# The two float16 parts of the attention maxima: converted from SBUF and turned by VectorE's 32x32 transposition, in place of a TensorE product into a score bank

## The chip, the cores and the metric

The kernel runs on one core of a Trainium2 chip. Such a core has five engines that run side by side, each with its own queue of instructions, and they wait for each other through semaphores: TensorE (PE, matrix products; its weight loads are listed as PEld), VectorE (DVE), ScalarE (ACT), GpSimd (POOL) and SyncE (SP), which here issues all DMAs. SBUF is the on-chip memory of 128 partitions. PSUM holds TensorE's results in eight banks of 128 partitions by 512 float32. The metric is the device time of one launch in microseconds (us), the median of several runs; less is better.

## The reference

One transformer block in its parallel form, for a sequence of 2048 rows of width 512, with 32 heads of 16 dimensions and a hidden width of 1792:

```python
xn = _layernorm(x, axis=-1)
# attention
qkv = (xn @ wqkv)                       # split into q, k, v of 32 heads of 16
scores = einsum("bhqd,bhkd->bhqk", q, k) * (16 ** -0.5)
p = softmax(scores, axis=-1)
attn = einsum("bhqk,bhkd->bhqd", p, v)  # heads side by side again, then @ wo
# dense part
h = gelu(xn @ w1 + b1)
mlp = h @ w2 + b2
return x + attn_out + mlp
```

The softmax needs, for each query and head, the maximum of its 2048 scores before the exponentials can be taken. It is that maximum which the change concerns.

## The kernel before

Products in float32 accuracy are made of float16 parts: a value is split into a high part and the rest, and three products (high x high, high x rest, rest x high) are added up. For attention, `kst` and `qst` hold, for each head, a stack of 64 rows: 48 rows of such parts (16 dimensions, three each), and at the end rows 62 and 63. In `kst` these two rows hold the constant 1024 (`MROW`). In `qst` they hold, for each query, the high and the low float16 part of -maximum / 1024. So a product over all 64 rows is the score less the maximum of its query, and a product over the first 62 rows is the score alone.

The work of attention is cut into 32 tiles t: a group g of 4 heads (`NG` = 8) by a block qb of 512 queries (`NQB` = 4). A tile is worked in 16 units, and a unit is the step of the outer loop (`unit`). In each unit the kernel works at three places at once:

- `s_half` (L169 by way of `tiled`, and L257), four times a unit, for unit u: 128 queries by 512 keys of one head. The 62-row product goes into one of three score banks (tag S, name `pS`), and VectorE takes its maximum over the keys into a column of `mt`. These banks are used in turn. A fourth block waits until the reduction of the first has ended.
- `e_half` (L169, L302), four times a unit, for unit u - 19 (`LEAD`): 128 keys by 512 queries of one head, the 64-row product into a bank of tag T (name `pT`), and ScalarE takes its exponential into `pe`.
- `v_half` (L169) for a unit a little further back: the product of the exponentials with v, into `pV`. Beside it, `dense` runs some products of the projections or of the dense part, into `pD`. Both use one half of TensorE's rows each.

When the last of the 16 units of a tile is done, `s_end` reduces `mt` (64 values a query partition) to `mneg`, 16 columns (4 heads by 4 blocks of 128 queries): the negative maxima, with the queries on the partitions (L268). They are needed with the queries along the free dimension, in rows 62 and 63 of `qst`, three units later, when `e_half` comes to this tile. The way there is `store`, which runs in the middle of the next unit, after its first two score blocks and first `v_half`: TensorE multiplies `mneg` with a unit matrix (L275), which turns it, into a score bank taken with `banks("S")`; VectorE makes the high part and the rest from PSUM (`mhl`, L278 and L279); two DMAs write them to `m_d` in DRAM (L282) and four DMAs read them into the rows of `qst`, one for each head (L287). `mneg` has 32 columns for this product, of which 16 are cleared once at the start by GpSimd.

From the second tile on, all queues keep the order in which the code writes the instructions (`manual_schedule`). Ahead of it, for the layer norm, the first projections and the score blocks of the first tile, a scheduler orders them. Work that should come some units later is put into `queue` by `later`, and `tick` runs it at a unit's end. GpSimd's work goes through `pooled` and a budget of time for each unit: among it the normalisation of a finished tile (L358 to L360) and the pieces of the GELU (L1019 to L1027), which read and write SBUF. SyncE's queue, too, is in order: a DMA whose source isn't ready holds all that come behind it.

Of the kernel before, what the change touches and what calls it, by code (L numbers as in the profile page):

```python
# [8 lines left out]
F32 = mybir.dt.float32  # L9
F16 = mybir.dt.float16  # L10
I32 = mybir.dt.int32
AF = mybir.ActivationFunctionType
ALU = mybir.AluOpType
AX = mybir.AxisListType
# [3 lines left out]
P = 128  # L18
S = 2048
# [8 lines left out]
NQB = S // QB  # L28
NG = H // 4
# [13 lines left out]
MROW = 1024.0  # L43
# [4 lines left out]
def layer_kernel(ctx: ExitStack, tc: tile.TileContext, x, wqkv, wo, w1, b1, w2, b2, out):  # L48
    nc = tc.nc
    x = x.flatten_outer_dims()  # L50
    out = out.flatten_outer_dims()

    def pool(stack, name, bufs=1, space=None, side=None):
        kw = {k: v for k, v in (("space", space), ("side", side)) if v is not None}
        return stack.enter_context(tc.tile_pool(name=name, bufs=bufs, **kw))

    const = pool(ctx, "const")
    work = pool(ctx, "work")
    ps = pool(ctx, "ps", space=PSUM)
    dram = pool(ctx, "dram", space=DRAM)  # L60
# [4 lines left out]
    w1_d = dram.tile([NF // 2, P, 2, 2, NC, P], F16, name="w1_d")  # L65
    w2_d = dram.tile([P, 2, NF, D], F16, name="w2_d")
    acc_d = dram.tile([S, D], F32, name="acc_d")
    m_d = dram.tile([NG * NQB, 16, 2, P], F16, name="m_d")
    ot_d = dram.tile([D, 2, S], F16, name="ot_d")
    den_d = dram.tile([NG * NQB, 2, 4, QB], F32, name="den_d")  # L70

# [1 line left out]
    ident = const.tile([P, P], F32, name="ident")  # L73
# [19 lines left out]
    nc.gpsimd.memset(vv[:, :, H * VW:], 0.0)  # L93
    wo_s = const.tile([P, 2, NC, D], F16, name="wo_s")
    sexp = const.tile([P, 4], F32, name="sexp")

    mnegs = [const.tile([P, 32], F32, name=f"mneg{i}") for i in range(2)]
    for m in mnegs:
        nc.gpsimd.memset(m, 0.0)


    free_banks = {"S": [0, 1, 2], "T": [3, 4, 5], "D": [6], "V": [7]}
# [1 line left out]
    def bank_tile(k, tag):  # L104
        return ps.tile([P, QB], F32, tag=f"B{k}", bufs=1, name="p" + tag)

    def banks(tag):
        k = free_banks[tag].pop(0)
        free_banks[tag].append(k)
        return bank_tile(k, tag)  # L110
# [48 lines left out]
    def given(engine, ns):  # L159
        backlog[engine] += ns  # L160
# [17 lines left out]
    def leave(user, goes_on):  # L178

        p = newest.pop(user, None)  # L180
        if p is not None and goes_on:
            p.then_inc(turns, 1)
            tc.no_tile_sem_insts.add(p.ins.name)
            counted[0] += 1
            left.append(p)

    def enter():

        if left:
            goal[0] = f"turn{counted[0]}"  # L190
            for p in left:
                tc.add_to_no_dep_group(goal[0], p.ins)
            left.clear()
# [9 lines left out]
    def fetch_scale(m):  # L203

        scale_of[m] = nc.scalar.alloc_register(f"sexp{m}")
        nc.scalar.reg_load(scale_of[m], sexp[0:1, m:m + 1].bitcast(I32))

    mt_of, ptiles, pv_of, stores = {}, {}, {}, {}
    queue, slot = [], [0]

    def later(n, fn, local=False):
# [21 lines left out]
    def tick():  # L233
        run_due()
        run_steps()
        slot[0] += 1
# [8 lines left out]
    def s_half(u, n):  # L245

        t, i = divmod(u, 16)
        g, qb = divmod(t, NQB)
        qt, kb = divmod(i, 4) if t else (i % 4, i // 4)
        if t not in mt_of:  # L250
            mt_of[t] = work.tile([P, 4, 4, 4], F32, name="mt", bufs=2)
        ks, qs = kst[g % 2], qst[g % 2]
        p, a = divmod(n, 2)
        r = slice(64 * a, 64 * a + 62)
        s = banks("S")
        tiled(None, s, qs[p][qb][r, qt * P:(qt + 1) * P], ks[p][kb][r, :], True, True)
        nc.vector.reduce_max(mt_of[t][:, n, qt, kb:kb + 1], s, axis=AX.X)  # L257
        given("dve", 600)

    def s_end(u):  # L260

        t, i = divmod(u, 16)
        if i < 15:
            return
        g, qb = divmod(t, NQB)
        qs = qst[g % 2]
        mneg = mnegs[t % 2]
        nc.vector.tensor_reduce(mneg[:, :16], mt_of[t].rearrange("p h t k -> p (h t) k"), axis=AX.X, op=ALU.max, negate=True)  # L268
        given("dve", 220)

        def store():

            pt = banks("S")
            for a in range(2):
                nc.tensor.matmul(pt[32 * a:32 * a + 32, :64], mneg[64 * a:64 * a + 64, :],  # L275
                                 ident[64 * a:64 * a + 64, 64 * a:64 * a + 64], start=True, stop=True)
            mhl = work.tile([64, 2, 64], F16, name="mhl", bufs=2)
            nc.vector.tensor_scalar_mul(mhl[:, 0], pt[:64, :64], 1.0 / MROW)  # L278
            nc.vector.scalar_tensor_tensor(mhl[:, 1], pt[:64, :64], 1.0 / MROW, mhl[:, 0], op0=ALU.mult, op1=ALU.subtract)  # L279
            given("dve", 300)  # L280
            for a in range(2):
                nc.sync.dma_start(m_d[t, :, :, 64 * a:64 * a + 64], mhl[32 * a:32 * a + 16])  # L282
            for p in range(2):
                for a in range(2):
                    h = 2 * p + a
                    dst = qs[p][qb][64 * a + 62:64 * a + 64, :].rearrange("r (t q) -> r t q", q=P)
                    nc.sync.dma_start(dst, m_d[t, 4 * h:4 * h + 4].rearrange("t r q -> r t q"))  # L287

        stores[t] = store

    def e_half(u, n):

        p, a = divmod(n, 2)
        t, kt = divmod(u, 16)
        g, qb = divmod(t, NQB)
        st = banks("T")
        r = slice(64 * a, 64 * a + 64)
        k0 = (kt % 4) * P
        tiled(None, st, kst[g % 2][p][kt // 4][r, k0:k0 + P], qst[g % 2][p][qb][r, :], True, True)
        pe = work.tile([P, QB], F32, name="pe", bufs=12)  # L300
        ptiles[u, n] = pe
        nc.scalar.activation(pe, st, AF.Exp, scale=scale_of[g // 2])  # L302
        given("act", 520)

    def v_half(u, a):

        t, kt = divmod(u, 16)
        g, qb = divmod(t, NQB)
        if kt == 0 and a == 0:
            pv_of[t] = hold("V", "S")  # L310
        pv = pv_of[t][0]
        r = slice(64 * a, 64 * a + 64)
        for h in (2, 3, 0, 1):
            c = (4 * g + h) * VW
            product("V", pv[32 * h:32 * h + 32, :], vv[r, kt, c:c + 32], ptiles[u, h][r],
                    start=(kt == 0 and a == 0), stop=(kt == 15 and a == 1))
# [249 lines left out]
    def burst(gen, n):  # L566

        while n > 0 and (f := group(gen)) is not None:
            if not f.usable():
                break  # L570
            f.product(2)
            n -= 1
            ended()

    def dense(gen, side):

        f = group(gen)
        for _ in range(0 if f is None else f.pace[pos[0] % 2]):
            if not f.usable(side):
                return  # L580
            f.product(side)
# [25 lines left out]
    def spare(gen, side):  # L607

        if extra[0] is None and not spent[0]:
            f = next(gen, 0)  # L610
            spent[0] = f == 0
            extra[0] = Halves(f) if f else None
        if extra[0] is not None:
            extra[0].product(side)
            if extra[0].at == extra[0].n:
                extra[0] = None
# [16 lines left out]
    def unit(gen):  # L633


        u = pos[0]
        e = u - LEAD
        if e >= 0 and e % (2 * NQB * 16) == 0 and e < NU:
            fetch_scale(e // (2 * NQB * 16))
        if u == LEAD and cur[0] is not None:  # L640
            burst(gen, cur[0].left())
        pos[0] += 1
        for a in range(2):
            for b in range(2 * a, 2 * a + 2):
                if u < NU:
                    s_half(u, b)
                elif u > NU:
                    spare(gen, b % 2)
                if 0 <= e < NU:
                    e_half(e, b ^ 1)  # L650
            if u < LEAD:
                burst(gen, LFILL[u - 16] // 2)
            if e >= 0:
                enter()

                w, r = (e - 2, 1) if a == 0 else (e - 1, 0)
                live = 0 <= w < NU
                new = r == 0 and w % 16 == 0
                if live and not new:
                    v_half(w, r)  # L660
                dense(gen, 1 - r)
                if live and new:
                    v_half(w, r)

                for user, goes_on in (("V", live and not (r == 1 and w % 16 == 15)),
                                      ("D", cur[0] is not None and not cur[0].over())):
                    leave(user, goes_on)
                for k in backlog:
                    backlog[k] = max(0, backlog[k] - HALF)
                if live and r == 1:  # L670
                    v_end(w)
                ended()

            if a == 0 and u % 16 == 0 and u // 16 - 1 in stores:
                stores.pop(u // 16 - 1)()
        if u < NU:
            s_end(u)
        tick()
# [549 lines left out]
```

## Time and profile before

| | |
|---|---|
| median of 3 runs | 1525.09 us (1520.38 to 1526.5) |
| the profiled execution, its own time | 1520.55 us |
| span of its profile | 1518.8 us |
| busy: TensorE, VectorE, ScalarE, GpSimd | 1489.5, 1402.2, 1245.6, 664.5 us |
| mean granted TensorE clock | 0.996 of full speed |
| L257, the reductions of score blocks | 2048 of 684 ns |
| L268, L278, L279 on VectorE, 32 each | 219, 209, 217 ns |
| L275 on TensorE, 128 instructions | 216 ns |
| DMA: share of 16 engines' span | 25.4% |

A row of the groups names the line of the code, the engine, the operation, what is written from what, the shape and the count; then the busy time in us and the mean of one in ns; then the engine's idle time just before, with what ended it. Busy times overlap: the next instruction of an engine may start before the last one is recorded as ended, so that the sum of the durations is more than the busy time. A row of the timeline gives the start and the length in us, and in square brackets the idle time ahead of it and what ended it. "x2" says that neighbouring instructions of one kind are merged into one row.

### The profile page before, as it was taken

Reading aid. Unit: us, or ns where it says so; the run is one execution under the profiler, and the core shown is the slowest. Engines: PE = TensorE matmul, PEld = TensorE weight load, DVE = VectorE, ACT = ScalarE, POOL = GpSimd, SP = SyncE. Lnnn points to the kernel's source line nnn. Section 1 sums busy time; section 2 is a strip of 40 time slices with the busy share of each in tenths; the row PEclk is TensorE's granted clock in tenths of the full one; section 3 lists DMA queues with packets and bytes.
Section 4 is the critical chain, followed back from the end, with each engine's and each line's share of the span. In section 5 each row is a group of like instructions: output and inputs, shape, how many; then the busy total and the mean of one; then the engine's idle time right before and its main releaser. Section 6 shows DMA issues by size and latency. Waiting matters only on the chain.

```text
span 1518.8 us, 86848 instructions
## 1 busy us (share of the span) xinstructions
PE 1489.5 (98%) x39407; PEld 815.9 (54%) x39407; DVE 1402.2 (92%) x2367; ACT 1245.6 (82%) x2318; POOL 664.5 (44%) x686
## 2 busy tenths in 40 slices
PE   8999999999999999999999999999999999999998
PEld 3434555555555555555555555555555555555553
DVE  7899989999999999999999999999999999999933
ACT  5327778899988888898888898988888898888884
POOL 4113597547771112777411167751116775211110
PEclk9999999999999999999999999999999999999998
DMA  6454567542122201121011211122101201121422
GB/s 208 127 155 158 166 219 211 180 126 77 58 69 66 61 26 42 36 84 50 23 49 41 66 42 40 36 78 63 34 25 56 77 27 29 50 60 50 136 65 95
DMA packets 113674, 123.76 MB, mean 81 GB/s; under 512 B 24988, under 2 KB 85276, under 8 KB 113304
## 3 DMA queue, kind: packets, MB, share of 16 engines
q1 hardware_dynamic: 113304, 118.21, 25.4%
q8 instruction: 308, 5.05, 1.4%
q14 instruction: 62, 0.51, 0.1%
HBM read 80.61 MB, written 37.34 MB: 78 GB/s over the span
## 4 chain that ended last, share of the span: by engine, by line
PE 79%; DVE 16%; issue 2%; ACT 2%; DMA 1%; POOL 0%; SPq 0%; POOLq 0%
PE pV L169 23%; PE pD L169 19%; PE pT L169 17%; PE pS L169 16%; DVE mt L257 13%; PE pT L435 1%; PE pD L435 1%; DVE amx L709 1%; ACT pe L302 1%; ACT t L1014 1%; PE pT L528 1%; PE pV L528 0%; DMA m_d<-mhl 0%; DMA xs<-in_A_x_dram 0%; DMA wch<-in_B_w_dram 0%
## 5 line engine op out<-in xcount | busy, mean ns | idle before, releaser
L257 DVE TENSOR_REDUCE mt<-pS 128x1 f32<-128x512 f32 x2048 | 1304.5, 684 | 52.5 <-PE pS L169 34.8
L302 ACT ACTIVATE pe<-pT 128x512 f32<-128x512 f32 x2048 | 1100.8, 599 | 162.9 <-PE pS L169 78.6
L169 PE MATMUL pV<-pe,vv 64*32 64x512 f32 x8192 | 1076.3, 595 | 0.1
L169 PE MATMUL pT<-qst,kst 64*32 64x512 f16 x8192 | 718.3, 378 | 8.8 <-ACT pe L302 7.9
L169 PE MATMUL pS<-kst,qst 62*32 62x512 f16 x8192 | 624.3, 378 | 5.2 <-DVE mt L257 3.6
L169 PEld LDWEIGHTS <-kst 64*32 64x32 f16 x8192 | 285.7, 91 | 203.9 <-issue 103.6
L169 PEld LDWEIGHTS <-qst 62*32 62x32 f16 x8192 | 273.3, 92 | 206.3 <-issue 58.2
L169 PE MATMUL pD<-w_s,g 64*32 64x512 f16 x5376 | 364.6, 376 | 0.0
L169 PE MATMUL pD<-xb,wc 64*32 64x512 f16 x5376 | 360.9, 377 | 0.0
L169 PEld LDWEIGHTS pV<-pe,vv 64*32 64x32 f32 x8192 | 181.0, 105 | 88.3 <-PE pV L169 4.3
L1070 POOL TENSOR_TENSOR xa<-xa,yt 128x512 f32<-128x512 f32 x16 | 20.5, 1282 | 319.0 <-ACT yt L1068 319.0
L169 PEld LDWEIGHTS <-wc 64*32 64x32 f16 x5376 | 116.9, 91 | 41.6
L169 PEld LDWEIGHTS <-g 64*32 64x32 f16 x5376 | 112.2, 91 | 45.3
L169 PE MATMUL pD<-xt,wqk_h 64*32 64x512 f16 x2016 | 134.7, 377 | 1.7 <-issue 1.5
L1025 POOL TENSOR_TENSOR t<-hh 128x512 f32<-128x512 f32 x56 | 58.3, 1041 | 132.7 <-ACT hh L1045 121.8
L358 POOL TENSOR_TENSOR osb<-osb,rb 128x512 f32<-128x512 f32 x31 | 39.9, 1287 | 135.1 <-DMA rb<-den_d 76.0
L1027 POOL TENSOR_TENSOR t<-t,hh 128x512 f32<-128x512 f32 x56 | 71.9, 1284 | 4.7
L1020 POOL TENSOR_TENSOR t<-t,hh 128x512 f32<-128x512 f32 x56 | 71.8, 1281 | 4.7
L1022 POOL TENSOR_TENSOR g<-t,g 128x512 f16<-128x512 f32 x56 | 65.2, 1165 | 4.7
L169 PEld LDWEIGHTS <-wqk_h 64*32 64x32 f16 x2016 | 47.5, 92 | 23.4 <-issue 6.2
L169 PE MATMUL pD<-wo_s,oc 64*32 64x512 f16 x828 | 54.5, 378 | 0.0
L1045 ACT ACTIVATE hh<-pD,b_s,fac 128x512 f32<-128x512 f32 x56 | 43.6, 779 | 9.4 <-PE pT L169 3.3
(141 smaller groups left out, 862.4 us busy)
## 6 DMA issues: line engine op xcount, KB each, us to landing
wch<-in_B_w_dram SPq DMA_DIRECT2D x28, 512.0 KB
wc<-w_d SPq DMA_DIRECT2D x56, 256.0 KB
qk_d<-stg SPq DMA_DIRECT2D x32, 256.0 KB
rb<-den_d SPq DMA_DIRECT2D x124, 64.0 KB
w_d<-wsp SPq DMA_DIRECT2D x28, 256.0 KB
kst<-qk_d SPq DMA_DIRECT2D x128, 48.0 KB
qst<-qk_d SPq DMA_DIRECT2D x128, 48.0 KB
xs<-in_A_x_dram SPq DMA_DIRECT2D x16, 256.0 KB
```

The costliest lines, as they stand in the source:

```text
L169: p = nc.tensor.matmul(*args, **kw)
L257: nc.vector.reduce_max(mt_of[t][:, n, qt, kb:kb + 1], s, axis=AX.X)
L302: nc.scalar.activation(pe, st, AF.Exp, scale=scale_of[g // 2])
L358: pooled((1280, lambda: nc.gpsimd.tensor_tensor(osb, osb, rb, op=ALU.mult)), (620, lambda: nc.gpsimd.tensor_scalar(ot[:, 0], osb, 1.0, 0.0 ...
L435: nc.tensor.matmul(self.bank, lhs, rhs, start=start, stop=self.last and self.over())
L528: nc.tensor.matmul(pj, xt[:, i, c, t * P:(t + 1) * P], wh[j][:, c, :], start=(n == 0), stop=(n == 11))
L1020: (1280, lambda: nc.gpsimd.tensor_tensor(t1, t1, hh, op=ALU.mult)),
L1022: (1160, lambda: nc.gpsimd.tensor_tensor(g[:, 1, f, :], t1, g[:, 0, f, :], op=ALU.subtract)),
L1025: pooled((1040, lambda: nc.gpsimd.tensor_tensor(t1, hh, hh, op=ALU.mult)), (620, lambda: nc.gpsimd.tensor_scalar(t1, t1, 1.0, 1.0 / GELU_A ...
L1027: (1280, lambda: nc.gpsimd.tensor_tensor(t1, t1, hh, op=ALU.mult)),
L1045: nc.scalar.activation(hh, hp, AF.Identity, scale=scale, bias=bias)
L1070: add = lambda: nc.gpsimd.tensor_tensor(xa, xa, yt, op=ALU.add)
```

## The change

`mneg` has 16 columns only and comes from the working pool, in two buffers. Directly behind the reduction L268, in `s_end`, VectorE makes the two float16 parts from `mneg` in SBUF: the high part into columns 0 to 15 of `mh`, the rest into columns 16 to 31. Then VectorE transposes `mh` in blocks of 32 by 32, so that each block of 32 partitions (32 queries) of `mc` holds 32 rows (2 parts by 16 columns) by 32 queries. Four DMAs, one for each such block, write them to `m_d`, whose layout is now part, column, query; and four DMAs read them into `qst`, each now two rows of 512 in one piece. The DMAs are put on SyncE's queue at the same place, ahead of what `tick` issues at that unit's end. The product with the unit matrix, its score bank, the function `store` and its call in the middle of the next unit go, and so do GpSimd's two clearings.

```diff
--- before.py
+++ after.py
@@ -65,7 +65,7 @@
     w1_d = dram.tile([NF // 2, P, 2, 2, NC, P], F16, name="w1_d")
     w2_d = dram.tile([P, 2, NF, D], F16, name="w2_d")
     acc_d = dram.tile([S, D], F32, name="acc_d")
-    m_d = dram.tile([NG * NQB, 16, 2, P], F16, name="m_d")
+    m_d = dram.tile([NG * NQB, 2, 16, P], F16, name="m_d")
     ot_d = dram.tile([D, 2, S], F16, name="ot_d")
     den_d = dram.tile([NG * NQB, 2, 4, QB], F32, name="den_d")
 
@@ -93,10 +93,6 @@
     nc.gpsimd.memset(vv[:, :, H * VW:], 0.0)
     wo_s = const.tile([P, 2, NC, D], F16, name="wo_s")
     sexp = const.tile([P, 4], F32, name="sexp")
-
-    mnegs = [const.tile([P, 32], F32, name=f"mneg{i}") for i in range(2)]
-    for m in mnegs:
-        nc.gpsimd.memset(m, 0.0)
 
 
     free_banks = {"S": [0, 1, 2], "T": [3, 4, 5], "D": [6], "V": [7]}
@@ -205,7 +201,7 @@
         scale_of[m] = nc.scalar.alloc_register(f"sexp{m}")
         nc.scalar.reg_load(scale_of[m], sexp[0:1, m:m + 1].bitcast(I32))
 
-    mt_of, ptiles, pv_of, stores = {}, {}, {}, {}
+    mt_of, ptiles, pv_of = {}, {}, {}
     queue, slot = [], [0]
 
     def later(n, fn, local=False):
@@ -264,29 +260,22 @@
             return
         g, qb = divmod(t, NQB)
         qs = qst[g % 2]
-        mneg = mnegs[t % 2]
-        nc.vector.tensor_reduce(mneg[:, :16], mt_of[t].rearrange("p h t k -> p (h t) k"), axis=AX.X, op=ALU.max, negate=True)
+        mneg = work.tile([P, 16], F32, name="mneg", bufs=2)
+        nc.vector.tensor_reduce(mneg, mt_of[t].rearrange("p h t k -> p (h t) k"), axis=AX.X, op=ALU.max, negate=True)
         given("dve", 220)
 
-        def store():
-
-            pt = banks("S")
+        mh, mc = (work.tile([P, 32], F16, name=x, bufs=2) for x in ("mh", "mc"))
+        nc.vector.tensor_scalar_mul(mh[:, :16], mneg, 1.0 / MROW)
+        nc.vector.scalar_tensor_tensor(mh[:, 16:], mneg, 1.0 / MROW, mh[:, :16], op0=ALU.mult, op1=ALU.subtract)
+        nc.vector.transpose(mc, mh)
+        rows = m_d[t].rearrange("j c q -> (j c) q")
+        for b in range(4):
+            nc.sync.dma_start(rows[:, 32 * b:32 * b + 32], mc[32 * b:32 * b + 32])
+        for p in range(2):
             for a in range(2):
-                nc.tensor.matmul(pt[32 * a:32 * a + 32, :64], mneg[64 * a:64 * a + 64, :],
-                                 ident[64 * a:64 * a + 64, 64 * a:64 * a + 64], start=True, stop=True)
-            mhl = work.tile([64, 2, 64], F16, name="mhl", bufs=2)
-            nc.vector.tensor_scalar_mul(mhl[:, 0], pt[:64, :64], 1.0 / MROW)
-            nc.vector.scalar_tensor_tensor(mhl[:, 1], pt[:64, :64], 1.0 / MROW, mhl[:, 0], op0=ALU.mult, op1=ALU.subtract)
-            given("dve", 300)
-            for a in range(2):
-                nc.sync.dma_start(m_d[t, :, :, 64 * a:64 * a + 64], mhl[32 * a:32 * a + 16])
-            for p in range(2):
-                for a in range(2):
-                    h = 2 * p + a
-                    dst = qs[p][qb][64 * a + 62:64 * a + 64, :].rearrange("r (t q) -> r t q", q=P)
-                    nc.sync.dma_start(dst, m_d[t, 4 * h:4 * h + 4].rearrange("t r q -> r t q"))
-
-        stores[t] = store
+                h = 2 * p + a
+                nc.sync.dma_start(qs[p][qb][64 * a + 62:64 * a + 64, :],
+                                  m_d[t, :, 4 * h:4 * h + 4].rearrange("j t q -> j (t q)"))
 
     def e_half(u, n):
 
@@ -671,8 +660,6 @@
                     v_end(w)
                 ended()
 
-            if a == 0 and u % 16 == 0 and u // 16 - 1 in stores:
-                stores.pop(u // 16 - 1)()
         if u < NU:
             s_end(u)
         tick()
```

## The prediction

> **What bounds the kernel now.** I read the page's head first, then its chain of waits and the costliest groups.
>
> ```profile
> span 1518.8 us, 86848 instructions
> PE 1489.5 (98%) x39407; PEld 815.9 (54%) x39407; DVE 1402.2 (92%) x2367; ACT 1245.6 (82%) x2318; POOL 664.5 (44%) x686
> PE 79%; DVE 16%; issue 2%; ACT 2%; DMA 1%; POOL 0%; SPq 0%; POOLq 0%
> L257 DVE TENSOR_REDUCE mt<-pS 128x1 f32<-128x512 f32 x2048 | 1304.5, 684 | 52.5 <-PE pS L169 34.8 <-PE pT L169 4.1
> ```
>
> TensorE and VectorE run side by side, both nearly full: TensorE carries most of the chain, but every score block goes through one L257 reduction, 2048 of them, and a score bank is free only when its reduction has ended. VectorE cannot be held up for long before TensorE stands. The changed code runs at the 32 tile changes, so I opened one of them in the timeline (rows of all engines, in order of time; the parts that matter).
>
> ```profile
> 851.56 0.42 PE L169 MATMUL pS<-kst,qst 62*32 62x512 f16 x8
> ...
> 852.04 0.22 DVE L268 TENSOR_REDUCE mneg<-mt 128x16 f32<-128x64 f32 x1
> 852.17 1.28 DVE L257 TENSOR_REDUCE mt<-pS 128x1 f32<-128x512 f32 x2
> 852.26 1.28 POOL L358 TENSOR_TENSOR osb<-osb,rb 128x512 f32<-128x512 f32 x1 [19.32 <-DMA rb<-den_d]
> 853.37 0.21 DVE L278 TENSOR_SCALAR mhl<-pS 64x64 f16<-64x64 f32 x1
> 853.51 0.40 PE L169 MATMUL pS<-kst,qst 62*32 62x512 f16 x4 [0.16 <-DVE mt L257]
> 853.61 0.22 DVE L279 SCALAR_TENSOR_TENSOR mhl<-pS,mhl 64x64 f16<-64x64 f32 x1
> 853.62 0.62 POOL L359 TENSOR_SCALAR ot<-osb 128x512 f16<-128x512 f32 x1
> 853.75 6.41 DVE L257 TENSOR_REDUCE mt<-pS 128x1 f32<-128x512 f32 x10
> 853.85 1.22 SPq L282 DMA_DIRECT2D m_d<-mhl  x2
> 854.58 0.41 PE L169 MATMUL pS<-kst,qst 62*32 62x512 f16 x8
> 856.30 1.16 SPq L287 DMA_DIRECT2D qst<-m_d  x4
> 857.16 0.42 PE L169 MATMUL pS<-kst,qst 62*32 62x512 f16 x8
> 859.94 0.40 PE L169 MATMUL pT<-qst,kst 64*32 64x512 f16 x4
> ```
>
> A unit starts with two score blocks. The one at the tile change takes 854.58 - 851.56 = 3.02 us, the next 857.16 - 854.58 = 2.58. So a tile change costs 0.44 us more than another unit, about 14 us over 32. Its place is visible: the fourth score block starts at 853.51, after a wait for a reduction. The maxima's product L275 has taken one of the three score banks, so the fourth block needs the bank of the second block, whose reduction ended at 852.17 + 1.28 = 853.45.
>
> **The change, part by part.**
>
> *TensorE and the bank.* L275 goes (32 times). I cost that at nothing: TensorE already ran dry at 853.51 - 0.16 = 853.35 and waited for VectorE, so a shorter queue ahead of the wait doesn't end it earlier. What does change is which reduction is waited for: without L275's bank the fourth block needs the bank of the first block, one reduction earlier.
>
> *VectorE, unhindered.* Before, L268 is followed at once by two reductions, and L278 and L279 come behind them. Now three small operations that depend on each other stand directly behind L268, ahead of every reduction of the new tile; the instruction listing of the changed kernel shows mneg, mh, mh, mc, then the reductions. A dependent operation starts 0.03 us after its input's end (853.37 + 0.21 = 853.58, L279 at 853.61). An operation that isn't dependent starts 0.09 ahead of the end (852.04 + 0.22 = 852.26, reduction at 852.17). For the new forms the nearest rows are small operations from SBUF:
>
> ```profile
> L138 DVE TENSOR_SCALAR fac<-sc_c x6: 135/160/386, 11.4 to 179.0; 128x2 int32<-128x2 int32 x4, 128x1 int32<-128x1 int32 x1, 128x10 int32<-128x10 int32 x1
> L268 DVE TENSOR_REDUCE mneg<-mt x32: 205/220/221, 107.0 to 1452.0; 128x16 f32<-128x64 f32 x32
> L346 DVE RECIPROCAL dn<-dn x31: 333/334/337, 191.1 to 1476.2; 64x32 f32<-64x32 f32 x31
> ```
>
> (minimum/median/maximum ns.) I take 0.16 for the first product (the 160), 0.17 for the second (between the 160 and L279's 0.22, with a quarter of L279's columns) and 0.19 for the transposition, which no row shows: its bounds are L138's shortest, 0.14, and L346's 0.33, which also has 32 columns; I stay near the small ones, since L268 reads 64 columns in 0.22. From L268's start to the first reduction: 0.22 + 0.03 + 0.16 + 0.03 + 0.17 + 0.03 + 0.19 - 0.09 = 0.74 us. The first reduction then runs from 852.78 to 853.46 (0.684 long), and the fourth block starts 0.06 behind it (as 853.51 follows 853.45), at 853.52. Before: 853.51. So the two things cancel: +0.01 a tile change, with the bounds of the transposition and of the second product -0.05 to +0.2 (0.33 for 0.19, and 0.22 for 0.17). I take +0.5 us in all, bounds -1.5 and +6.
>
> *VectorE, hindered by GpSimd.* L278 and L279 read PSUM. The new products read SBUF, and the second has two SBUF inputs (mneg, mh). In this trace such operations stand still while GpSimd works:
>
> ```profile
> 151.68 2.14 POOL L939 TENSOR_TENSOR wsp<-wch,wsp 128x1024 f16<-128x1024 f32 x1
> 151.80 2.03 DVE L959 TENSOR_TENSOR gs<-gs,fac 128x1 f32<-128x1 f32 x1
> 154.48 0.40 PE L169 MATMUL pS<-kst,qst 62*32 62x512 f16 x4 [1.39 <-DVE mt L257]
> ...
> 178.27 1.13 POOL L937 TENSOR_SCALAR wch<-wch,inv 128x1024 f32<-128x1024 f32 x1
> 179.03 0.39 DVE L138 TENSOR_SCALAR fac<-sc_c 128x2 int32<-128x2 int32 x1
> ```
>
> L959 handles one column and lasts 2.03 us: it ends at 153.83, with GpSimd's L939 (153.82). TensorE pays: its next score block waited 1.39 us for a reduction. L138, one SBUF input, two columns, ends with L937 (179.42 against 179.40) in 0.39 instead of 0.16. The reciprocal L346 and the reduction L268, one input each, keep their length everywhere, though GpSimd runs beside many of them (L508, shown below, from 206.16 to 207.33, beside the L268 of 206.57). The second product is of L959's kind, the first of L138's.
>
> How often does GpSimd run there? Windows of 0.1 us, 0.25 behind the start of each of the 32 L268, GpSimd alone (first and last of the busy ones, and the sum):
>
> ```profile
> 206.82:206.92 0.10, 0.10 (x1) 1.00 1.10 410
> ...
> 1324.75:1324.85 0.10, 0.10 (x1) 1.00 0.00 0
> ...
> sum 3.20, POOL 1.80; mean POOL 0.06
> 206.16 1.17 POOL L508 TENSOR_TENSOR stg<-pf,stg 128x512 f16<-128x512 f32 x1
> 1323.90 1.29 POOL L358 TENSOR_TENSOR osb<-osb,rb 128x512 f32<-128x512 f32 x1
> ```
>
> 1.80 of 3.20: in 18 of 32. What is left of the running operation, from the window's start: 207.33 - 206.82 = 0.51 at the first, 1325.19 - 1324.75 = 0.44 at the last, 853.54 - 852.29 = 1.25 at the one shown. Read alike, the 18 add up to 15.1 us for the first product. Then the second: it tries some 0.18 later, and at 16 of the 18 GpSimd's next operation has begun by then (L359 at 853.62, 0.08 behind L358). If it holds that one too, 854.24 - 853.72 = 0.52 here and 12.5 us over the 16. If the first product isn't held at all, the second alone waits 11.7 us. So 11.7 to 27.6; I take the first wait whole and half of the second, 15.1 + 6.2 = 21.3, since L138 shows VectorE done 0.02 behind GpSimd's end and a start between two operations is a race. Every such wait passes on to the fourth block one to one, for the 0.74 has used up its room.
>
> [...]
>
> *ScalarE.* While TensorE stands, ScalarE catches up.
>
> ```profile
> PE pT L169 <- ACT pe L302: 7.9, 20, 0.7
> PEld L169 <- DMA qst<-m_d: 1.1, 1, 1.1
> 113.84 0.37 SPq L492 DMA_DIRECT2D qk_d<-stg  x1
> 119.86 2.06 ACT L302 ACTIVATE pe<-pT 128x512 f32<-128x512 f32 x4
> ```
>
> TensorE waits 7.9 us for it in all; I take a quarter of that back, -2.
>
> *The DMA queue.* Eight issues a tile for six: four writes instead of two, 0.61 each (1.22 for two), +1.22, and four reads as before. They start from 852.04 + 0.83 (transposition's end) instead of 853.85, 0.98 earlier, so the last read is issued 0.24 later, at about 857.7, for a first use at 859.94. What is queued behind (weights, stores of the same slot) has units of room. Held products move the rows and their use alike. Cost nothing; without that room it would be 0.24 a tile, 7 us. The first tile is scheduled, not written out: there the reads stand behind L492 on the queue, at 113.84, and the first exponential is at 119.86, so nothing waits. Two cleared tiles less on GpSimd at the start: nothing.
>
> **Sum.** 0.5 + 21.3 - 2 = +19.8 us. The profiled execution took 1520.55 us; that gives 1540. The median of the three runs shown, 1525.09, lies 4.5 above it; on it, 1545.
>
> **The rivals.**
> *No change:* these forms are not held (16 columns of two types aren't L138's case, scalar_tensor_tensor not L959's). Against it stand both rows. Then +0.5: 1526. Chance 0.10.
> *Faster:* the three small operations are so short that the bank given back wins the tile change's 0.44 us. It decides where the chain from L268 falls under 0.49 us (a gain of 0.25 a change, 8 us); with 0.25 for L268 and its gap, 0.24 would be left for three operations whose like take 0.135 at least. Fully won: 0.44 x 32 = 14 us, 1511. Chance 0.04.
> *The rows come late:* the four small writes land later, and the exponential's products wait, as at the one wait of 1.1 us for qst<-m_d. From 859.94 back there are some 2 us behind the last issue, of which the landing takes part. If each tile waited 0.5 us: +16, 1541, and in addition to any hold. Chance 0.04.
>
> **How the numbers follow.** Held by GpSimd: 0.82, own range 1533 (11.7 + 0.5 - 4) to 1556 (27.6 + 0.5, and 3 us of scatter as between the runs). The range 1527 to 1559 takes in this, the late rows on top, and stops at the edge of no change. About 0.5% (7.6 us) is what a measurement of this kernel tells from none. Faster 0.05, same 0.11, slower 0.84.
>
> **What would show it.** Right: mh rows with medians far above their minimum, maxima over 1 us, ending with GpSimd's operations; TensorE's waits for L257's reductions grown by 15 us or more; unit lengths between tile changes unchanged. Wrong: mh rows all near 0.16, or waits for qst<-m_d in every tile. The weakest step is the half of the second wait.

## The result, and the profile after

The changed kernel takes 1541.3 us (median of 4 runs, 1540.2 to 1541.9) against 1525.3 us before on the same chip (4 runs, 1520.4 to 1526.5): a ratio of 1.0119, with a 95% interval of 1.0096 to 1.0142. It is slower, by 16 us. The prediction was 1545, between 1527 and 1559. One run named below, of the first experiment, took 1557.3 us at a mean granted clock of 0.945 where that kernel's other runs had 0.993 or more; the ratio leaves it out.

The head of the page of the changed kernel, the line of its chain by engine, and the costliest group of VectorE (the reductions of the score blocks, now L253):

```profile
span 1540.1 us, 86672 instructions
PE 1490.2 (97%) x39279; PEld 811.2 (53%) x39279; DVE 1420.1 (92%) x2399; ACT 1247.4 (81%) x2318; POOL 663.0 (43%) x684
PE 74%; DVE 20%; issue 2%; ACT 2%; DMA 1%; POOL 0%; SPq 0%; ACTq 0%; DVEq 0%; POOLq 0%
L253 DVE TENSOR_REDUCE mt<-pS 128x1 f32<-128x512 f32 x2048 | 1297.5, 683 | 52.8 <-PE pS L165 31.6
```

TensorE's busy time hardly moved (1489.5 before), the span grew by 21.3 us. VectorE is 17.9 us busier, and its share of the chain rose from 16% to 20%, though its 2048 reductions take what they took. So VectorE spends time on something small, and TensorE waits for it. The view of TensorE's waits (total in us, times, longest) says where:

```profile
PE pS L165 <- DVE mt L253: 25.6, 34, 2.1
PE pT L165 <- ACT pe L291: 8.3, 20, 1.1
```

The first of these rows was, before:

```profile
PE pS L169 <- DVE mt L257: 3.6, 14, 1.4
```

It grew by 22.0 us, about as much as the span. A wait for `qst<-m_d`, the way of the rows through DRAM, has no row any more.

The view of the tile `mh` (minimum/median/maximum in ns, then the first and last start) shows what VectorE does:

```profile
L268 DVE TENSOR_SCALAR mh<-mneg x32: 156/382/1262, 108.3 to 1474.0; 128x16 f16<-128x16 f32 x32
L269 DVE SCALAR_TENSOR_TENSOR mh<-mneg,mh x32: 157/176/1193, 108.9 to 1474.2; 128x16 f16<-128x16 f32 x32
L270 DVE STREAM_TRANSPOSE mc<-mh x32: 194/211/214, 109.6 to 1474.4; 128x32 f16<-128x32 f16 x32
```

The same 16 columns take 0.16 us or 1.26 us. The transposition is the same every time. Three tile changes from the timeline show when, in order of time: one where both products are held, one where the first alone is, and one where neither is. (L1014 is a piece of the GELU, L347 and L348 belong to the normalisation: L1027, L358 and L359 before.)

```profile
387.70 0.22 DVE L264 TENSOR_REDUCE mneg<-mt 128x16 f32<-128x64 f32 x1
387.86 1.29 POOL L1014 TENSOR_TENSOR t<-t,hh 128x512 f32<-128x512 f32 x1
387.96 1.22 DVE L268 TENSOR_SCALAR mh<-mneg 128x16 f16<-128x16 f32 x1
389.10 1.27 POOL L347 TENSOR_TENSOR osb<-osb,rb 128x512 f32<-128x512 f32 x1
389.21 1.19 DVE L269 SCALAR_TENSOR_TENSOR mh<-mneg,mh 128x16 f16<-128x16 f32 x1
390.57 2.44 DVE L253 TENSOR_REDUCE mt<-pS 128x1 f32<-128x512 f32 x4
391.27 0.40 PE L165 MATMUL pS<-kst,qst 62*32 62x512 f16 x4 [2.08 <-DVE mt L253]
...
739.53 1.29 POOL L347 TENSOR_TENSOR osb<-osb,rb 128x512 f32<-128x512 f32 x1
739.96 0.89 DVE L268 TENSOR_SCALAR mh<-mneg 128x16 f16<-128x16 f32 x1
740.88 0.17 DVE L269 SCALAR_TENSOR_TENSOR mh<-mneg,mh 128x16 f16<-128x16 f32 x1
740.91 0.64 POOL L348 TENSOR_SCALAR ot<-osb 128x512 f16<-128x512 f32 x1
...
864.59 0.42 PE L165 MATMUL pS<-kst,qst 62*32 62x512 f16 x8
865.06 0.22 DVE L264 TENSOR_REDUCE mneg<-mt 128x16 f32<-128x64 f32 x1
865.87 4.23 DVE L253 TENSOR_REDUCE mt<-pS 128x1 f32<-128x512 f32 x7
866.57 0.40 PE L165 MATMUL pS<-kst,qst 62*32 62x512 f16 x4 [0.31 <-DVE mt L253]
867.67 0.49 PE L165 MATMUL pS<-kst,qst 62*32 62x512 f16 x8
```

In the first, GpSimd's L1014 ends at 389.15 and the first product at 389.18. L347 had begun at 389.10, and the second product ends 0.03 behind that one as well (390.40 against 390.37). In the second, L347 ends at 740.82 and lets the first product go at 740.85; GpSimd's next operation begins at 740.91, and the second product, begun 0.03 before it, runs free in 0.17. In the third, GpSimd does nothing while the products run: the tile change takes 867.67 - 864.59 = 3.08 us, against 3.02 before.

Read like this over all 32 tile changes, with 0.175 us for a product that isn't held, the first product is held at 17, for 11.7 us in all; the second at 5, for 4.4 us.

One more thing came with it. The view of windows (us, TensorE busy, granted clock, DMA share, GB/s), in steps of 3.413 us: two in the first tile, then those behind the hold at 388 and around that at 695:

```profile
119.01:122.42 3.41, 2.17 (x49) 1.00 0.71 241
122.42:125.83 3.41, 3.41 (x64) 0.50 0.44 118
...
388.66:392.07 3.41, 1.33 (x44) 1.00 0.03 6
392.07:395.48 3.41, 3.41 (x68) 0.50 0.03 4
395.48:398.90 3.42, 3.42 (x104) 1.00 0.70 221
692.46:695.87 3.41, 2.50 (x68) 1.00 0.31 101
695.87:699.28 3.41, 2.23 (x68) 1.00 0.03 2
```

The stalls of TensorE behind 388 and at 695 are both 2.08 us long. Behind the first, the clock is halved for 3.41 us; behind the second it isn't. At two of the three tile changes with such a stall this happened (the other low stretch begins at 999.64). There the unit behind took 3.8 and 3.7 us instead of 2.6, and the tile change's own unit, whose end is slow too, 0.2 and 0.4 us more than at 695: about 1.5 us each, 3.0 us in all (two expectations below take 2.6). The low stretch at 122.42 lies in the first tile; the profile before has none there. The ladder of stalls, below, takes this up.

### The profile page after: what moved, and what is told of

Same layout as the page of the kernel before. It is cut to its first block, busy times and chain, and to the rows that moved or that the text cites. A ratio compares the mean times of both kernels' runs of the same rounds, so it can differ in the third digit from the quotient of the medians.

```text
span 1540.1 us, 86672 instructions
## 1 busy us (share of the span) xinstructions
PE 1490.2 (97%) x39279; PEld 811.2 (53%) x39279; DVE 1420.1 (92%) x2399; ACT 1247.4 (81%) x2318; POOL 663.0 (43%) x684
## 4 chain that ended last, share of the span: by engine, by line
PE 74%; DVE 20%; issue 2%; ACT 2%; DMA 1%; POOL 0%; SPq 0%; ACTq 0%; DVEq 0%; POOLq 0%
PE pV L165 22%; PE pD L165 18%; DVE mt L253 16%; PE pT L165 16%; PE pS L165 15%; DVE mh L268 1%; PE pT L424 1%; PE pD L424 1%; DVE amx L696 1%; ACT pe L291 1%; ACT t L1001 1%; DVE mh L269 1%; PE pT L517 1%; DVE mneg L264 0%; PE pV L517 0%
## 5 line engine op out<-in xcount | busy, mean ns | idle before, releaser
L253 DVE TENSOR_REDUCE mt<-pS 128x1 f32<-128x512 f32 x2048 | 1297.5, 683 | 52.8 <-PE pS L165 31.6
L165 PE MATMUL pS<-kst,qst 62*32 62x512 f16 x8192 | 627.1, 379 | 28.0 <-DVE mt L253 25.6
L347 POOL TENSOR_TENSOR osb<-osb,rb 128x512 f32<-128x512 f32 x31 | 39.8, 1284 | 141.1 <-DMA rb<-den_d 102.1
L1014 POOL TENSOR_TENSOR t<-t,hh 128x512 f32<-128x512 f32 x56 | 71.8, 1282 | 4.7
```

Of the source, the lines that this page charges most:

```text
L165: p = nc.tensor.matmul(*args, **kw)
L347: pooled((1280, lambda: nc.gpsimd.tensor_tensor(osb, osb, rb, op=ALU.mult)), (620, lambda: nc.gpsimd.tensor_scalar(ot[:, 0], osb, 1.0, 0.0 ...
L1014: (1280, lambda: nc.gpsimd.tensor_tensor(t1, t1, hh, op=ALU.mult)),
```

## The experiments

The theory (A): the two products from SBUF stand still while a GpSimd operation runs, VectorE passes the delay on to the fourth score block, and nothing else in the change costs much. The rivals: (B) the longer chain ahead of the tile's first reduction is what costs, held or not; (C) the rows reach `qst` late by the new way.

**One-input reductions in place of both products.** VectorE's reductions over SBUF kept their length before, beside GpSimd (L268: 205 to 221 ns in all 32). So the high part is made by a second reduction of `mt` straight to float16, and the rest as the sum of a pair, with `MROW` 1 instead of 1024. (`flat` is `mt` with its 64 columns in a row; the first column of `pair` is `mneg`.) Place, transposition and the eight DMAs are those of the changed kernel; the chain gets longer by one operation.

```diff
-MROW = 1024.0
+MROW = 1.0
...
-        nc.vector.tensor_scalar_mul(mh[:, :16], mneg, 1.0 / MROW)
-        nc.vector.scalar_tensor_tensor(mh[:, 16:], mneg, 1.0 / MROW, mh[:, :16], op0=ALU.mult, op1=ALU.subtract)
+        nc.vector.tensor_reduce(mh[:, :16], flat, axis=AX.X, op=ALU.max, negate=True)
+        nc.vector.tensor_reduce(pair[:, :, 1], mh[:, :16].unsqueeze(2), axis=AX.X, op=ALU.max, negate=True)
...
+            nc.vector.tensor_reduce(mh[:, 16:], pair, axis=AX.X, op=ALU.add)
```

> The changed kernel with its place, transposition and eight DMAs kept, but without its two products: the high part comes from a second reduction of the 64 maxima straight to float16 (the constant 1024 is 1), the rest from two reductions with one SBUF input each. Four small dependent reductions and the transposition stand where two products and the transposition stood. Theory A (GpSimd holds the products): the trace of the changed kernel has 11.7 us of holds in the first product, 4.4 us in the second and some 2.6 us in two tiles with a low clock; these go, and one more dependent operation costs some 0.1 us a tile, 3 us: 1525 us, and no VectorE operation at a tile change longer than 0.25 us. Rival B (three dependent operations ahead of the reductions cost it, whoever executes them): 1541 us or some 3 us more. Rival C (the eight DMAs and the later rows): 1541 us.

Measured: 1527.17 us (12 runs), ratio to before 1.0024 [1.0012, 1.0035]. Its tile view:

```profile
L270 DVE TENSOR_REDUCE mh<-mt x32: 207/209/211, 107.4 to 1460.1; 128x16 f16<-128x64 f32 x32
L271 DVE TENSOR_REDUCE pair<-mh x32: 158/171/173, 108.1 to 1460.3; 128x16 f32<-128x16 f16 x32
L273 DVE TENSOR_REDUCE mh<-pair x32: 173/186/189, 108.8 to 1460.5; 128x16 f16<-128x32 f32 x32
```

No operation is ever held: minimum and maximum lie within 0.02 us, in the same place where the products took up to 1.26. 14 of the 16 us are gone, with a chain that is longer. (B) and (C) expected 1541 and fall as the main cause. What (B) is worth shows, too: TensorE's waits for the reductions of score blocks are 14.2 us here, 25.6 in the changed kernel and 3.6 before, and each undisturbed tile is 0.18 us longer than before, 5.8 us over 32, of the order of the 3.5 us that are left between the medians (1523.66 for the kernel before on that chip).

**Only the first product replaced.** This tells whether a `scalar_tensor_tensor` with two SBUF inputs is held by itself, which no run had shown.

```diff
-        nc.vector.tensor_scalar_mul(mh[:, :16], mneg, 1.0 / MROW)
+        nc.vector.tensor_reduce(mh[:, :16], flat, axis=AX.X, op=ALU.max, negate=True)
         nc.vector.scalar_tensor_tensor(mh[:, 16:], mneg, 1.0 / MROW, mh[:, :16], op0=ALU.mult, op1=ALU.subtract)
```

> Only the first product of the changed kernel goes (the high part is a second reduction of the maxima, the constant 1024 is 1); the second, with two SBUF inputs, stays. Theory A: the second product now meets the GpSimd operation that held the first one, so most of the 11.7 us of holds move to it, one hold a tile instead of two, and no stall reaches 2 us: 1535 us, with maxima of the second product over 1 us. [...] Rivals B and C: 1541 us.

Measured: 1531.39 us (7 runs), 1.0058 [1.0041, 1.0076]. Its tile view:

```profile
L269 DVE TENSOR_REDUCE mh<-mt x32: 207/209/213, 107.7 to 1462.2; 128x16 f16<-128x64 f32 x32
L270 DVE SCALAR_TENSOR_TENSOR mh<-mneg,mh x32: 162/260/1091, 108.4 to 1462.4; 128x16 f16<-128x16 f32 x32
```

Now the second product meets the running operation itself, and is held: at 17 tile changes, for 9.2 us in all by the same reading. The kernel is only 4 us slower than the one with reductions alone, since its chain has one operation less (an undisturbed tile takes 41.46 us instead of 41.67). So each product is held by itself, and in the changed kernel the first one takes most of the wait for both.

**The products spread among the new tile's reductions.** If the wait is passed on because VectorE has no room ahead of the first reduction, one of the three operations behind each of the first three reductions should fit.

```diff
         given("dve", 600)
+        if between and u % 16 == 0:
+            between.pop(0)()
...
+        between.extend((part1, part2, part3))
```

(`part1` and `part2` are the two products, `part3` the transposition with its DMAs.)

> The two products and the transposition of the changed kernel as they are, but not in one piece ahead of the new tile's reductions: one behind each of its first three reductions; the DMAs follow the transposition. Theory A: what the three operations cost without a hold (0.44 us a tile, 14 us) goes, since each then costs some 0.08 us in VectorE's order; the holds stay, 10 to 16 us less the 0.3 us a tile that the score banks can take: 1519 to 1524 us. Rival B: 1511 us, since nothing stands ahead of the reductions any more. Rival C: 1541 us or later, since the rows come 2 us later.

Measured: 1533.55 us (10 runs), 1.0055 [1.0038, 1.0073]. The expectation missed by 10 us. TensorE's waits:

```profile
PE pT L165 <- DMA qst<-m_d: 9.3, 11, 2.4
...
PE pS L165 <- DVE mt L254: 6.6, 16, 1.4
```

The waits for the reductions fall from 25.6 to 6.6, as intended, but the holds stay (6.6 and 4.1 us by the same reading), and now the transposition and the writes come behind them. TensorE waits for late rows 11 times. This is the rival (C) of the prediction, brought about by the remedy.

**The one-input reductions, spread.** Neither held nor bunched:

```diff
+        def part1():
+            nc.vector.tensor_reduce(pair[:, :, 1], mh[:, :16].unsqueeze(2), axis=AX.X, op=ALU.max, negate=True)
...
+        def part2():
...
+                nc.vector.tensor_reduce(mh[:, 16:], pair, axis=AX.X, op=ALU.add)
+            nc.vector.transpose(mc, mh)
...
+        between.extend((part1, part2))
```

> Reductions in place of the products, as in the kernel without products, and spread: the high part behind the maxima, one reduction behind the first of the new tile's reductions, the rest and the transposition behind the second. Theory A and rival B: no hold, no piece of dependent work, no score bank taken: the 0.44 us of a tile change go too, 1512 us, faster than before. Rival C: the rows are written 1.2 us later than in the changed kernel and reach the exponentials late by up to 0.5 us a tile: 1525 us or more.

Measured: 1522.39 us (12 runs), 0.9990 [0.9977, 1.0003]: not to be told from before, where 1512 was expected. The timeline at a tile change, the first blocks of three units:

```profile
812.76 0.42 PE L165 MATMUL pS<-kst,qst 62*32 62x512 f16 x8
815.33 0.88 PE L165 MATMUL pS<-kst,qst 62*32 62x512 f16 x8
818.18 0.41 PE L165 MATMUL pS<-kst,qst 62*32 62x512 f16 x8
```

The tile change's unit takes 815.33 - 812.76 = 2.57 us, like any other: the 0.44 us is won. The next one takes 818.18 - 815.33 = 2.85 instead of 2.58. VectorE has five small operations more to do than in other units (0.22, 0.21, 0.16, 0.17 and 0.21 us, some 0.7 without their overlaps), and it has hardly any room: seven block reductions in a row took 4.23 us in the changed kernel (the row at 865.87), so a unit's four take 2.42 of 2.57 us. That is an argument: the trace shows only 0.10 us of the 0.27 as a wait for VectorE, at 815.82. And the rival (C) isn't quite absent, for TensorE waits 1.5 us, in 5 waits, for late rows. The reading that the place of the work only moves the wait, and less work removes it, is put to the test by the last experiment.

**GpSimd's normalisation three units later.** The changed kernel as it is, but the operations that were most often found at the tile change are queued for another time.

```diff
-        at = (1, 3, 6, 7, 9, 12) if t < (NG - 1) * NQB else (1, 2, 5, 6, 7, 8)
+        at = (1, 3, 6, 7, 9, 15) if t < (NG - 1) * NQB else (1, 2, 5, 6, 7, 8)
```

> The changed kernel with one number altered: GpSimd's normalisation of a finished tile (three operations of 3.1 us together) is queued three units later, so that it runs behind the tile change instead of beside it. VectorE's operations, their order and the DMAs of the maxima stay. Theory A (GpSimd holds the products): of the 16.1 us of holds, 8.0 us were by these three operations, and without them no stall reaches 2 us, so the 2.6 us under the low clock go too: 1531 us, give or take 3, with the holds by the GELU's operations left. Rivals (VectorE's own added work; the DMAs): 1541 us.

Measured: 1539.2 us (6 runs), 1.0094 [1.0074, 1.0115], where 1531 was expected. The holds fall from 17 and 5 to 12 and 7, 16.1 to 12.3 us. The timeline at the same tile change as above shows why not more:

```profile
387.95 1.29 POOL L1014 TENSOR_TENSOR t<-t,hh 128x512 f32<-128x512 f32 x1
388.05 1.22 DVE L268 TENSOR_SCALAR mh<-mneg 128x16 f16<-128x16 f32 x1
389.22 0.70 POOL L1006 TENSOR_SCALAR t<-t,gs 128x512 f32<-128x512 f32 x1
389.31 0.63 DVE L269 SCALAR_TENSOR_TENSOR mh<-mneg,mh 128x16 f16<-128x16 f32 x1
390.81 0.40 PE L165 MATMUL pS<-kst,qst 62*32 62x512 f16 x4 [1.53 <-DVE mt L253]
```

GpSimd's next operation in the queue, a piece of the GELU, takes the free place directly behind L1014 and holds the second product. It is shorter (0.70 instead of 1.27), the stall is 1.53 instead of 2.08 us, and the clock stays, as far as it shows: the score products behind it take 0.40 and 0.39 us, and the mean granted clock is 0.994 against 0.992. Other operations moved to other tile changes: behind one that had been free the tile grew by 1.9 us, and at one where the first product alone had been held the second now is too (1.0 us). The last tiles grew by up to 2.2 us in units away from the tile change; 1.6 us of it is a wait of TensorE for ScalarE that ends at 1412.54, whose cause stays open.

**A ladder of stalls.** The question is when the clock falls. The kernel before gets, behind the maxima of each tile from the fifth on, a reduction whose result nothing reads, longer with every second tile; VectorE is late by its length, and TensorE stands.

```diff
+        if t > 3:
+            probe = work.tile([P, 1], F32, name="probe", bufs=2)
+            nc.vector.tensor_reduce(probe, vv[:, 0:t // 2 - 1, 0:256], axis=AX.XY, op=ALU.max)
```

> The kernel before with one reduction more behind the maxima of each tile from the fifth on, whose result nothing reads; it grows with the tile, from 256 to 3584 columns (0.4 to 3.9 us, two tiles of each length), so that TensorE stands ever longer. If the granted clock falls because TensorE stood for some 2 us or more, it is 1.00 behind all stalls below 2 us and falls to 0.5 for about 3.4 us behind all those above 2.2 us, and products of 0.38 us last 0.65. If the two low stretches of the changed kernel had another cause, the clock stays at 1.00 at any length, or falls at any. Time in all, at 0.4 to 3.9 us a tile for 28 tiles: some 55 us more than before, and 1.3 us more for each low stretch.

Measured in one execution: 1589.17 us, mean clock 0.986. Behind the first 15 of the 28 probes the clock stayed at 1.00. Behind the other 13, with stalls of 1.92 to 3.5 us, it fell 9 times and 4 times not: behind 1.92 it did, behind one of 1.95 and one of 3.29 it didn't. No threshold of the stall's length fits that. But the low stretches lie on a grid of 3.413 us: in the changed kernel those between 100 and 1500 us begin at 122.42, 392.07 and 999.64, 79 and 178 such steps apart, and last one step each; here three of the nine begin at 961.85, 1190.54 and 1477.26, 67 and 84 steps apart, and last one, two and one. The view of windows in steps of that grid (us, TensorE busy, granted clock, DMA share, GB/s):

```profile
958.44:961.85 3.41, 1.30 (x48) 1.00 0.01 2
961.85:965.26 3.41, 3.41 (x65) 0.50 0.03 4
...
1006.22:1009.63 3.41, 1.58 (x48) 1.00 0.00 0
1009.63:1013.05 3.42, 3.42 (x112) 1.00 0.05 7
...
1187.13:1190.54 3.41, 1.56 (x44) 1.00 0.00 0
1190.54:1193.95 3.41, 2.48 (x40) 0.50 0.03 6
1193.95:1197.37 3.42, 3.42 (x66) 0.50 0.01 2
...
1426.06:1429.47 3.41, 1.65 (x52) 1.00 0.02 5
1429.48:1432.89 3.41, 1.70 (x48) 1.00 0.00 0
1432.89:1436.30 3.41, 3.41 (x108) 1.00 0.05 10
...
1473.85:1477.26 3.41, 0.38 (x8) 1.00 0.00 1
1477.26:1480.67 3.41, 3.22 (x51) 0.50 0.04 7
```

What tells these cases apart is how much of a stall falls into one step. Where a step at full clock has TensorE busy for 0.38, 1.30 or 1.56 us of 3.41, the next one is at half clock; where it has 1.58, 1.65 or 1.70, it isn't. The stall of 3.29 us at 1427.7 is cut in two by the grid, 1.77 and 1.52, and costs no clock. The same reading holds in the changed kernel: 1.33 us busy and then 0.50 at 388.66, but 2.50 and 2.23 around 695, where the grid cuts the stall. It doesn't cover every case. A step at half clock with 2.48 us busy is followed by another at half clock (1190.54, above), and in the first tile of the changed kernel 2.17 us at full clock were followed by one (119.01). Why, no run here shows.

**Less work: the high part alone.** The low part of the maxima is left out (its row of `qst` stays zero). The softmax is then shifted by the rounded maximum, in numerator and denominator alike, so it keeps its value. VectorE reduces `mt` straight to float16 and transposes that, behind the first reduction of the new tile; four writes of 16 rows, four reads of one row. `MROW` is 1 here too.

```diff
-        nc.vector.tensor_reduce(mneg, mt_of[t].rearrange("p h t k -> p (h t) k"), axis=AX.X, op=ALU.max, negate=True)
+        mh, mc = mhs[t % 2], work.tile([P, 32], F16, name="mc", bufs=2)
+        nc.vector.tensor_reduce(mh[:, :16], mt_of[t].rearrange("p h t k -> p (h t) k"), axis=AX.X, op=ALU.max, negate=True)
...
+        between.extend((part1,))
```

> What the experiments so far point to: VectorE's chain at the tile change as short as it can be. The maxima are reduced straight to float16 (the constant 1024 is 1), and the low part is left out: its row of the stack stays zero, since a softmax is the same for any constant close to the maximum, if all keys of a query use the same one. One reduction and, behind the first reduction of the new tile, the transposition; four DMAs of 16 rows, four reads of one row. No product, so no hold; no score bank; two short operations, 0.26 us in VectorE's order. Theory A with what the spread reductions showed (VectorE's 0.15 us of room a unit bears some 0.3 us a tile): the 0.44 us of a tile change go almost wholly: 1512 us. If the tile change costs its 0.44 us for another reason than VectorE's work and the bank: 1522 us as with the spread reductions.

Measured: 1514.26 us (6 runs), 0.9936 [0.9913, 0.9958]. It beats both kernels, and less work is what the argument above asked for; the bytes of the rows are halved with it, so the two aren't separated. Then the same once more, and beside it on the same chip the same with the transposition directly behind the reduction, which tests the room that the prediction gave a short chain:

```diff
-        between.extend((part1,))
+        part1()
```

> hi_only once more, on the same chip as hi_direct (the low part is left out). 1514 again, ratio to before 0.9936 within 0.003, if that gain isn't a chip's own; tile change units of 2.55 us as other units.

> As hi_only (the low part of the maxima is left out, so row 63 of qst stays zero), but the transposition stands directly behind the reduction to float16, ahead of every reduction of the new tile. Theory (a tile change has room for a short chain on VectorE, and wins the bank's 0.44 us where the chain fits): from the start of the reduction to the first block's reduction 0.22 + 0.03 + 0.20 - 0.09 = 0.36 us, so the fourth block, which needs that reduction's bank, starts 0.36 + 0.68 + 0.06 = 1.10 us behind; with hi_only it started 1.02 behind (851.18 to 852.20) without a wait. So 0.08 us a tile change above hi_only, 2.6 us: 1517, and waits of the fourth block of 0.1 us. Rival (the gain comes from the place behind the first reduction, and anything ahead of it costs its whole length): 0.22 us a tile change, 7 us: 1521 or more.

Measured: 1512.78 us (6 runs), 0.9932 [0.9908, 0.9955], and 1513.34 us (4 runs), 0.9933 [0.9907, 0.9959]. In the first, the unit of the tile change at 848 takes 850.53 - 847.98 = 2.55 us, as expected. The timeline of the second at an undisturbed tile change:

```profile
848.38 0.42 PE L168 MATMUL pS<-kst,qst 62*32 62x512 f16 x8
848.86 0.22 DVE L267 TENSOR_REDUCE mh<-mt 128x16 f16<-128x64 f32 x1
849.95 0.40 PE L168 MATMUL pS<-kst,qst 62*32 62x512 f16 x4
851.05 0.49 PE L168 MATMUL pS<-kst,qst 62*32 62x512 f16 x8
```

The fourth block starts 1.09 us behind the maxima's reduction (1.10 was worked out), and the unit takes 2.67 us for 3.02. An undisturbed tile is 41.13 us long, against 40.99 with the transposition behind the first reduction and 41.48 before. These 0.14 us a tile are not to be seen in the medians. The rival, 1521 or more, falls: the place matters little once the chain is short.

## Why the prediction was right

The forecast's case came about: slower, held by GpSimd. On its profiled execution the sum gave 1540; the one profiled now took 1541.9. On the median it gave 1545 against 1541.3: the execution profiled before was among the shortest of its kernel and the one profiled now is the longest of its four, so on medians the change costs 16.0 us, not 19.8. The steps, in their order:

- *TensorE and the bank, at nothing.* Right as far as it shows: a tile without a hold is 0.06 us longer than before. A gain of 10 us came only where the chain is short; no run separates the bank's share in it.
- *VectorE, unhindered: +0.01 a tile change, 0.74 us of chain.* Measured 865.87 - 865.06 = 0.81 us, and 0.06 a tile, about 2 us instead of 0.5. The transposition takes 0.21 us (0.19 taken), the gap of a dependent operation is 0.04. Within its bounds.
- *First product held: 18 of 32, 15.1 us.* The mechanism is shown, by the trace and by the kernel with reductions; measured 17 and 11.7. Two parts make up the difference. The working took the whole of what was left of GpSimd's operation, without taking off the 0.15 us or so that the product needs anyway (18 times, 2.6 us). And the 1.25 us read at the tile change shown in the prediction didn't occur: there L347 now starts 1.44 us behind the maxima's reduction, where its counterpart had started 0.22 behind.
- *Second product: up to 12.5, half taken, 6.2.* The weakest step by its own word. Measured 4.4 us at 5 tile changes. The half was a guess; what decides is whether GpSimd's next operation begins before the last one has ended. At 4 of the 17 it does and the second product is held too; with a pause of 0.09 us, as between L347 and L348, or with nothing behind, it runs free. At a fifth change, with the first product free, a GpSimd operation began just ahead of the second.
- *ScalarE, -2.* Wrong, though small: its wait is 8.3 us now, 7.9 before.
- *The DMA queue and the rows, nothing.* Right: no wait for `qst<-m_d` is left, and the rival of late rows didn't occur until the spread products made it.
- *Left out:* the clock, 3.0 us at the two tile changes. No term of the sum spoke of it.

Summed for the profiled executions: 11.7 + 4.4 + 3.0 + 2 = 21.1, beside the 21.3 us by which the span grew. It doesn't close as well as that looks. The first tile, with its own low stretch of the clock, is another 1.4 us longer (53.08 us between its reduction to `mneg` and the next, 51.67 before), and not every hold is passed on whole, as the forecast had it: behind the holds of 1.46 us at 1215.99 the tile grew by 0.87 us only (44.99 for 44.12).

That the forecast's +19.8 lies so near the 21.3 is in part luck. Its two holds were 5.2 us too large (15.1 + 6.2 against 11.7 + 4.4); what it took too small or left out is 6.5 us (VectorE 1.5, ScalarE 2, the clock 3.0).

What was to be seen was seen: the first product's median (382) far above its minimum, maxima of more than 1 us that end with GpSimd's operations, the waits for reductions up by 22.0. Units between tile changes kept their length, but for those at half clock. Only the second product's median (176) doesn't show its holds; its maximum does.

Both forms are held, with up to 1.26 and 1.19 us for operations of 0.16. The forecast's upper figure, with the second product held at 16 of its 18 tile changes, was 27.6 us for the two; measured are 16.1. At 13 of the 17 tile changes the second product ran free once GpSimd's operation had ended, and the first waits were 3.4 us shorter than the forecast had them.

## What to carry to other kernels

Before moving small VectorE work from PSUM to SBUF, look at what GpSimd does at that moment: here a product of 0.16 us lasted up to 1.26, as long as GpSimd's operation of 1.3, and a reduction with one input was a substitute that wasn't held. Of a bank or an engine given back, ask whether the chain that replaces it fits into the room of the engine that is next to full; here moving the work about won nothing (ratio 0.9990), and leaving out the low part won 10 us. When an operation is moved out of the way on an in-order queue, ask what comes forward into its place.

## What was not expected of the hardware

The low stretches of TensorE's granted clock lie on a grid of 3.413 us: in the changed kernel they begin 79 and 178 such steps apart (122.42, 392.07, 999.64). Between 150 and 1490 us of that kernel two steps at full clock have TensorE busy for 1.33 us, and half clock follows on both; all others have 1.9 or more, and it follows on none. In the ladder it follows on steps with 0.38, 1.30 and 1.56 us, and not on those with 1.58, 1.65 and 1.70. So of three stalls of the same 2.08 us two cost some 1.5 us more and one cost nothing, by where the grid cuts them. The step at 119.01 (2.17 us busy, and half clock behind it) shows that it doesn't hold near the start.

A product that was held ended 0.02 to 0.03 us behind GpSimd's operation, at all 22 holds (389.18 against 389.15), and its successor was free where GpSimd paused for as little as 0.08 us (650.35 to 650.43).
